# Order of a kernel's first transfers: a weight block ahead of the keys, two more ahead of the values and queries

## The chip, the core and the metric

The kernel runs on one core of a Trainium2 chip. The metric is device time in microseconds (us) of one execution. The engines are named as the profile names them: PE (matmuls, with PEld for its weight loads), DVE, ACT, POOL, and SP, which here issues every DMA.

## The reference, cut to what matters

```python
def _attn_ref(q, k, v, p):                   # 8 batches, 8 heads, 576 tokens, 64 wide; p: 32 rows
    p_packed = sm_attn(p, k, v)              # 32 packed rows attend over keys and values
    out = sm_attn(q, p_packed, p_packed)     # the queries attend over the packed rows
...
x = attn_out, heads side by side             # 4608 x 512
h = x @ w_in                                 # w_in 512 x 1024, float64
solu = h * softmax(h)
ln = (solu - mu) / np.sqrt(var + 1e-06) * g_ln
x = (ln @ w_out).astype(np.float32)          # w_out 1024 x 512, float64
...
logits = x @ w_gate                          # 8 experts, the best one per token
out[mask] = gate_w * (np.maximum(xe @ w1[e], 0.0) @ w2[e])
```

Both w_in and w_out arrive as 64-bit floats: setup_inputs multiplies a float32 draw by a float64 scalar.

## The kernel before

The first half computes attention, h, the normalized solu and its product with w_out, batch by batch (8 batches); the second half runs the experts. Both matrices are fetched as raw words in eight blocks of 1 MB, `raw0` to `raw3` for w_in and `raw4` to `raw7` for w_out, and `decode` (L101 to L118) turns each into float32. A block costs DVE five passes: L111 cuts out sign and exponent, L113 joins them after ACT has shifted the exponent in between (L112), L114 and L115 assemble the mantissa, and L117 multiplies the two. For a block of w_out there follow two scalings and a rounding on ACT (L148, L149) and a subtraction on DVE (L150), which leave a high part `wo_hi` and a low part `wo_lo`.

The attention of a batch is a chain over the engines. `packed` makes scores of the packed rows (`s`, L164), their maxima on DVE (L166), exponentials on ACT (L172), transposes (L178, L181), the sum over the values (L187) and its transpose (L192). `scores2` scores the queries (L225 to L239; POOL scales at L239). `w_keys` multiplies the packed rows by w_in (L212) and splits the result in two on ACT (L213) and DVE (L214). `attnT` transposes the probabilities (L254) and splits them (L256 on ACT, L257 on DVE). `hidden` multiplies both into h, one PSUM tile per 128 tokens and two of those tiles in all (L273, twelve matmuls of 512 columns, a half after the other), takes maxima (L275, L276), exponentials (ACT, L281), the product with h (DVE, L283), squares (L286), and normalizes (L290 to L292). `lnT` transposes (L309 to L312) and `second` multiplies by w_out (L325). A PSUM tile of h comes free when L283 has read it.

For the first batch the order of these steps is written out by hand, in one string at L389. K issues p and the two halves of the keys, V issues the values and queries, F0 to F7 fetch the raw blocks, I0 to I3 and D0 to D3 decode them, and P, S, W, A, H, T, L, C are the steps above (`+` means the next batch). A scheduler then reorders the instructions of each engine, starting from that order, and fixes one order per engine; the engines wait for each other through semaphores. SP's DMAs are all on one queue and share eight completion lanes: the ninth DMA is not issued before the first has landed, and so on.

Of the kernel before, what the change touches and what calls it, by code (L numbers as in the profile page):

```python
# [27 lines left out]
P = 128  # L28
# [13 lines left out]
def fused_kernel(ctx: ExitStack, tc, qT, kT, pT, vm, vt, w_in, w_out, g_ln, w_gate, w1, w2, out):  # L42
    nc = tc.nc
    V, A, G, T, SY = nc.vector, nc.scalar, nc.gpsimd, nc.tensor, nc.sync
# [22 lines left out]
    with ExitStack() as ph:  # L67
# [318 lines left out]
                 "H": hidden, "T": lnT, "X": second, "G": gate, "F": fetch_block, "C": small,  # L386
                 "I": lambda _, i: decode_w_in(i, words[i]), "D": lambda _, i: decode_w_out(i, words[NC + i])}
        done = {("L", 0)}
        for step in ("K F0 F1 V F2 F3 C0 F4 F5 F6 P S0 S1 S2 I0 I1 I2 I3 W F7 A0 L+ H0 H1 D0 D1 T0 T1 D2 D3 A1 A2 C1").split():  # L389
            b = step.count("+")  # L390
            step = step.rstrip("+")
            steps[step[0]](b, *([int(step[1:])] if step[1:] else []))
            done.add((step, b))
# [153 lines left out]
```

## Time and profile before

| | us |
|---|---|
| median of 3 runs | 956.75 |
| lowest and highest | 956.64, 957.22 |
| the profiled execution | 957.72 |
| its span, first to last instruction | 956.0 |
| PE busy in the span | 911.4 |
| DVE busy in the span | 531.5 |

The profiled execution is the one from which every row below comes; 1.72 us of its time lie outside the span. Busy time is a sum over the whole span: it does not say which engine sets the pace of a stretch.

### The profile page before, as it was taken

How to read it: one execution, taken by the hardware profiler on the slowest of the kernel's cores; microseconds unless marked ns; L12 is line 12 of the kernel's file. 1: busy time of each engine (PE TensorE's matmuls, PEld its weight loads, DVE VectorE, ACT ScalarE, POOL GpSimd, SP SyncE). 2: the span in 40 equal slices, each digit the busy share in tenths (PEclk: the TensorE clock that was granted, in tenths of full speed). 3: DMA queues.
4: the chain of work that ended last, by engine and by line, in shares of the span. 5: the costliest groups of instructions: out<-in, count | busy, mean ns of one | idle time of the engine just before them, and what ended most of it. 6: DMA issues, size and time to landing. Idle time of an engine off the chain costs nothing.

```text
span 956.0 us, 18453 instructions
## 1 busy us (share of the span) xinstructions
PE 911.4 (95%) x7480; PEld 806.0 (84%) x7480; DVE 531.5 (56%) x1069; ACT 393.0 (41%) x774; POOL 74.3 (8%) x190
## 2 busy tenths in 40 slices
PE   4469999999999999999999999999999999999997
PEld 1237787887878878788878999999999999999997
DVE  5998667675666757667456253443435353535331
ACT  3366454554555545455345242323333232324230
POOL 0122111120111201112010000000000000000000
PEclk9779999999999999999999999999999999999999
DMA  9713132230322303201007145252535353433411
GB/s 341 273 44 103 51 102 102 58 145 2 103 101 63 140 2 100 101 2 51 2 25 238 54 129 171 85 190 89 178 90 183 94 174 114 155 122 99 130 45 52
DMA packets 41354, 102.89 MB, mean 108 GB/s; under 512 B 4464, under 2 KB 14256, under 8 KB 36144
## 3 DMA queue, kind: packets, MB, share of 16 engines
q1 hardware_dynamic: 41264, 101.65, 31.5%
q8 instruction: 61, 1.00, 0.4%
q14 instruction: 29, 0.24, 0.1%
HBM read 82.60 MB, written 19.04 MB: 106 GB/s over the span
## 4 chain that ended last, share of the span: by engine, by line
PE 89%; DVE 6%; DMA 2%; ACT 1%; issue 1%; SPq 0%; ACTq 0%; DVEq 0%
PE x L325 22%; PE y L468 21%; PE h L450 21%; PE h L273 11%; PE lt L309 3%; PE wb L212 2%; PE s L225 2%; PE lg L336 2%; PE s L164 2%; PE pp L187 1%; PE at L254 1%; DVE raw L115 1%; DVE pw L113 1%; DMA raw<-w_in 1%; DMA raw_0a<-w 1%
## 5 line engine op out<-in xcount | busy, mean ns | idle before, releaser
L325 PE MATMUL x<-lh,wo_hi 128*128 128x320 f32 (+1 forms) x512 | 156.1, 305 | 0.2 <-ACT x L327 0.2
L325 PE MATMUL x<-ll,wo_hi 128*128 128x320 f32 (+1 forms) x512 | 152.6, 298 | 0.0
L325 PE MATMUL x<-lh,wo_lo 128*128 128x320 f32 (+1 forms) x512 | 152.5, 298 | 0.0
L325 PEld LDWEIGHTS x<-lh,wo_hi 128*128 128x128 f32 x512 | 96.7, 189 | 18.8 <-issue 8.7
L325 PEld LDWEIGHTS x<-lh,wo_lo 128*128 128x128 f32 x512 | 96.8, 189 | 2.0 <-issue 0.8
L325 PEld LDWEIGHTS x<-ll,wo_hi 128*128 128x128 f32 x512 | 96.9, 189 | 1.6
L312 DVE TENSOR_TENSOR ll<-lt,lh 128x512 fp32r<-128x512 f32 (+1 forms) x80 | 50.4, 631 | 43.1 <-ACT lh L311 43.0
L273 PE MATMUL h<-wbh,ath 128*128 128x512 f32 (+1 forms) x160 | 67.8, 425 | 1.5 <-DVE e L283 0.8
L275 DVE TENSOR_REDUCE hm<-h 128x1 f32<-128x512 f32 (+1 forms) x80 | 54.5, 685 | 24.8 <-PE h L273 24.3
L273 PE MATMUL h<-wbh,atl 128*128 128x512 f32 (+1 forms) x160 | 65.1, 409 | 0.0
L273 PE MATMUL h<-wbl,ath 128*128 128x512 f32 (+1 forms) x160 | 64.2, 401 | 0.0
L311 ACT CAST lh<-lt 128x512 fp32r<-128x512 f32 (+1 forms) x80 | 43.2, 541 | 46.4 <-PE lt L309 46.1
L481 DVE TENSOR_TENSOR o<-y,gb 128x576 f32<-128x576 f32 (+1 forms) x33 | 24.4, 739 | 67.8 <-PE y L468 61.5
L283 DVE SCALAR_TENSOR_TENSOR e<-e,h 128x1024 f32<-128x1024 f32 (+1 forms) x40 | 48.6, 1216 | 21.1 <-ACT e L281 21.1
L281 ACT ACTIVATE e<-h,hm 128x1024 f32<-128x1024 f32 (+1 forms) x40 | 44.6, 1114 | 26.1 <-DVE hm L276 26.1
L286 ACT ACTIVATE sq<-e,mu 128x1024 bf16<-128x1024 f32 (+1 forms) x40 | 46.0, 1150 | 19.2 <-DVE e L283 14.2
L327 ACT COPY x<-x 128x256 f32<-128x256 f32 (+1 forms) x64 | 25.4, 397 | 57.3 <-PE x L325 56.9
L456 DVE SCALAR_TENSOR_TENSOR hl<-h,hh 128x576 fp32r<-128x576 f32 x64 | 47.9, 749 | 0.3 <-ACT hh L455 0.2
L309 PE MATMUL lt<-ident,e 128*128 128x128 f32 (+1 forms) x320 | 47.2, 267 | 0.5 <-DVE ll L312 0.5
L309 PEld LDWEIGHTS lt<-ident,e 128*128 128x128 f32 (+1 forms) x320 | 35.2, 140 | 9.5 <-issue 3.9
L455 ACT ACTIVATE hh<-h 128x576 fp32r<-128x576 f32 x64 | 41.3, 647 | 0.0
L292 DVE TENSOR_SCALAR e<-e,mu,va 128x1024 f32<-128x1024 f32 (+1 forms) x40 | 32.3, 807 | 11.1 <-POOL va L291 10.4
(229 smaller groups left out, 2090.7 us busy)
## 6 DMA issues: line engine op xcount, KB each, us to landing
k<-kT SPq DMA_DIRECT2D x16, 576.0 KB
q<-qT SPq DMA_DIRECT2D x8, 1152.0 KB
x2s<-x SPq DMA_DIRECT2D x8, 1152.0 KB
x<-x2s SPq DMA_DIRECT2D x8, 1152.0 KB
yT<-o SPq DMA_DIRECT2D x31, 288.0 KB
v<-vm SPq DMA_DIRECT2D x8, 1024.0 KB
raw<-w_in SPq DMA_DIRECT2D x4, 1024.0 KB
raw<-w_out SPq DMA_DIRECT2D x4, 1024.0 KB
```

The costliest lines, as they stand in the source:

```text
L273: T.matmul(ps[:rows, cols], s[x][:, t, g, :rows], s[y][:, g, cols], start=(n == 0), stop=(n == len(passes) - 1))
L275: V.tensor_reduce(nm[:rows, hf : hf + 1], ps[:rows, cols], axis=AX.X, op=ALU.max, negate=True)
L281: A.activation(er, psr, AF.Exp, bias=nm[:rows, 0:1], accum_out=z[:rows])
L283: V.scalar_tensor_tensor(er, er, 1.0 / FF, psr, op0=ALU.mult, op1=ALU.mult, accum_out=mu[:rows])
L286: A.activation(sq[:rows], er, AF.Square, bias=mu[:rows], scale=-float(FF), accum_out=va[:rows])
L309: T.transpose(ps[:, fc, :rows], e[:rows, (f0 + fc) * P : (f0 + fc + 1) * P], ident[:rows, :rows])
L311: A.copy(hi, ps[:, :, :rows])
L312: V.tensor_sub(s["ll", part][:, f0 : f0 + 4, t0 - p0 : t0 - p0 + rows], ps[:, :, :rows], f32(hi))
L325: T.matmul(ps[:, :pn], w[:, fc, cols], s[x, part][:, fc, :], start=(n == 0), stop=(n == 3 * NF - 1))
L450: T.matmul(ps[:, hf, :HALF], w[:, dc, :], x[:, dc, hf * HALF : (hf + 1) * HALF], start=(n == 0), stop=(n == 3 * NC - 1))
L456: V.scalar_tensor_tensor(lo, ps[:, :, :HALF], 0.0, f32(hi), op0=ALU.max, op1=ALU.subtract)
L468: T.matmul(ps[:, hf, :HALF], w[:, fc % 4, :], x[fc][:, hf, :], start=(n == 0), stop=(n == 3 * NF - 1))
```

## The change

The string at L389 gets another beginning. The first block of w_in is fetched ahead of p and the keys, and the second and third ahead of the values and queries; from F3 on the string is what it was.

```diff
-        for step in ("K F0 F1 V F2 F3 C0 F4 F5 F6 P S0 S1 S2 I0 I1 I2 I3 W F7 A0 L+ H0 H1 D0 D1 T0 T1 D2 D3 A1 A2 C1").split():
+        for step in ("F0 K F1 F2 V F3 C0 F4 F5 F6 P S0 S1 S2 I0 I1 I2 I3 W F7 A0 L+ H0 H1 D0 D1 T0 T1 D2 D3 A1 A2 C1").split():
```

Since a scheduler orders each engine's instructions anew, the change moves more than DMAs. On DVE, the start of the program (`s` are the scores of the packed rows, `pw` and `raw` belong to the decoding of a block; the difference, - before and + after):

```order
 L383 MEMSET lg 128x64
+L111 TENSOR_SCALAR pw_334<-raw_129 128x1024
+L113 SCALAR_TENSOR_TENSOR pw_334<-raw_129,pw_334 128x1024
 L166 TENSOR_REDUCE nm_0_158<-s_0_0_0_159 128x1
+L114 TENSOR_SCALAR raw_129<-raw_129 128x1024
+L115 SCALAR_TENSOR_TENSOR raw_129<-raw_129 128x1024
 L166 TENSOR_REDUCE nm_0_158<-s_0_0_1_165 128x1
+L117 SCALAR_TENSOR_TENSOR w_in_sb<-raw_129,pw_334 128x1024
 L168 TENSOR_TENSOR nm_0_158<-nm_0_158 128x1
-L111 TENSOR_SCALAR pw_334<-raw_135 128x1024
+L111 TENSOR_SCALAR pw_341<-raw_137 128x1024
 L174 SCALAR_TENSOR_TENSOR z_0_173<-z_0_173 128x1
```

The whole decoding of the first block now stands around the first maxima, where before it began after them.

On DVE, the place where the split of the first batch's `w_keys` ends (`wbl`, L214) and that of its transposed probabilities begins (`atl`, L257); before:

```order
L214 TENSOR_TENSOR wbl_363<-wb_0_1_378,wbh_362 128x512
L150 TENSOR_TENSOR wo_lo<-raw_150,wo_hi 128x1024
L117 SCALAR_TENSOR_TENSOR raw_152<-raw_152,pw_487 128x1024
L113 SCALAR_TENSOR_TENSOR pw_528<-raw_154,pw_528 128x1024
L214 TENSOR_TENSOR wbl_363<-wb_1_1_385,wbh_362 128x512
L257 TENSOR_TENSOR atl_395<-at_0_396,ath_394 128x512
L114 TENSOR_SCALAR raw_154<-raw_154 128x1024
L150 TENSOR_TENSOR wo_lo<-raw_152,wo_hi 128x1024
L111 TENSOR_SCALAR pw_539<-raw_392 128x1024
```

and after:

```order
L150 TENSOR_TENSOR wo_lo<-raw_152,wo_hi 128x1024
L117 SCALAR_TENSOR_TENSOR raw_154<-raw_154,pw_528 128x1024
L238 RECIPROCAL z_0_2_329<-z_0_2_329 64x8
L113 SCALAR_TENSOR_TENSOR pw_539<-raw_392,pw_539 128x1024
L214 TENSOR_TENSOR wbl_363<-wb_0_1_378,wbh_362 128x512
L214 TENSOR_TENSOR wbl_363<-wb_1_1_385,wbh_362 128x512
L114 TENSOR_SCALAR raw_392<-raw_392 128x1024
L150 TENSOR_TENSOR wo_lo<-raw_154,wo_hi 128x1024
L115 SCALAR_TENSOR_TENSOR raw_392<-raw_392 128x1024
L257 TENSOR_TENSOR atl_395<-at_0_396,ath_394 128x512
```

More of the decoding of w_out (`raw_150`, `raw_152`, `raw_154`, `raw_392` are its four blocks) now stands ahead of the L214s, and ahead of the first L257.

On DVE again, a little further on, up to the first two L283; before:

```order
L117 SCALAR_TENSOR_TENSOR raw_392<-raw_392,pw_539 128x1024
L283 SCALAR_TENSOR_TENSOR e_0_431,mu_0_434<-e_0_431,h_0_414 128x1024
L283 SCALAR_TENSOR_TENSOR e_1_462,mu_1_465<-e_1_462,h_1_445 128x1024
L174 SCALAR_TENSOR_TENSOR z_0_580<-z_0_580 128x1
L175 RECIPROCAL rz_563<-z_0_580 128x1
L290 TENSOR_SCALAR va_0_436<-va_0_436,hz_0_432 128x1
L292 TENSOR_SCALAR e_0_431<-e_0_431,mu_0_434,va_0_436 128x1024
L275 TENSOR_REDUCE hm_2_753<-h_2_752 128x1
L150 TENSOR_TENSOR wo_lo<-raw_392,wo_hi 128x1024
```

and after:

```order
L117 SCALAR_TENSOR_TENSOR raw_392<-raw_392,pw_539 128x1024
L275 TENSOR_REDUCE hm_0_415<-h_0_414 128x1
L275 TENSOR_REDUCE hm_1_446<-h_1_445 128x1
L166 TENSOR_REDUCE nm_0_565<-s_1_0_0_566 128x1
L257 TENSOR_TENSOR atl_395<-at_2_557,ath_394 128x2x64
L275 TENSOR_REDUCE hm_0_415<-h_0_414 128x1
L150 TENSOR_TENSOR wo_lo<-raw_392,wo_hi 128x1024
L276 TENSOR_TENSOR hm_0_415<-hm_0_415 128x1
L275 TENSOR_REDUCE hm_1_446<-h_1_445 128x1
L166 TENSOR_REDUCE nm_0_565<-s_1_0_1_572 128x1
L276 TENSOR_TENSOR hm_1_446<-hm_1_446 128x1
L168 TENSOR_TENSOR nm_0_565<-nm_0_565 128x1
```

The two L283 follow directly behind the last of these rows. The last L150 stood behind them and now stands ahead of them, and the maxima of h (L275), which were mixed with decoding before, now stand behind it.

## Rows read from the trace of the kernel before

**Rows 1.** The page, busy time of the span and DVE's busy tenths in 40 slices

```profile
PE 911.4 (95%) x7480; PEld 806.0 (84%) x7480; DVE 531.5 (56%) x1069; ACT 393.0 (41%) x774; POOL 74.3 (8%) x190
...
DVE  5998667675666757667456253443435353535331
```

**Rows 2.** PE's waits, 100 to 956 us: total, times, longest; the costliest

```profile
PE lgt L342 <- ACT lg L337: 0.9, 6, 0.2
```

**Rows 3.** Stages: PE, PEld, DVE, ACT, POOL busy; clock, DMA share, GB/s

```profile
0.00:5.00 5.00, 0.00 (x0) 0.00 (x0) 1.08 (x14) 1.59 (x2) 0.68 (x6) 1.00 0.50 145
5.00:10.00 5.00, 2.37 (x16) 0.43 (x16) 1.07 (x3) 0.68 (x3) 0.00 (x0) 1.00 1.04 385
10.00:15.00 5.00, 3.44 (x21) 1.32 (x21) 3.83 (x8) 3.22 (x6) 0.00 (x0) 1.00 1.06 406
...
20.00:25.00 5.00, 3.68 (x84) 2.47 (x83) 3.79 (x7) 2.10 (x4) 0.00 (x0) 1.00 1.02 410
```

**Rows 4.** Timeline of PE, its first matmuls: start, length, what, idle before

```profile
5.56 1.19 PE L164 MATMUL s<-k,p 64*32 64x288 f32 x8 [5.56 <-DMA k<-kT]
```

**Rows 5.** Timeline of DVE, six places

```profile
10.19 0.69 DVE L111 TENSOR_SCALAR pw<-raw 128x1024 uint16<-128x1024 uint16 x1 [0.96 <-DMA raw<-w_in]
...
47.23 0.92 DVE L237 TENSOR_SCALAR z<-z 64x8 f32<-64x8 f32 x1
...
49.92 0.63 DVE L214 TENSOR_TENSOR wbl<-wb,wbh 128x512 fp32r<-128x512 f32 x1
...
68.95 1.20 DVE L283 SCALAR_TENSOR_TENSOR e<-e,h 128x1024 f32<-128x1024 f32 x1
...
73.44 0.81 DVE L292 TENSOR_SCALAR e<-e,mu,va 128x1024 f32<-128x1024 f32 x1 [0.68 <-POOL va L291]
...
74.77 1.22 DVE L150 TENSOR_TENSOR wo_lo<-raw,wo_hi 128x1024 fp32r<-128x1024 f32 x1
```

**Rows 6.** Stages 52 to 75 us, columns as in rows 3

```profile
52.00:58.00 6.00, 5.38 (x14) 4.01 (x15) 6.00 (x8) 4.05 (x6) 2.42 (x1) 0.50 0.49 175
58.00:64.00 6.00, 5.54 (x33) 2.83 (x32) 6.00 (x10) 3.48 (x5) 0.00 (x0) 1.00 0.00 0
64.00:68.00 4.00, 0.00 (x0) 0.00 (x0) 4.00 (x9) 1.35 (x3) 0.06 (x1) 1.00 0.00 0
69.60:75.00 5.40, 5.40 (x15) 4.23 (x16) 3.71 (x10) 5.40 (x10) 0.97 (x4) 0.50 0.00 0
```

**Rows 7.** Timeline of PE, two starts after idle time

```profile
69.59 1.17 PE L178 MATMUL a1t<-ident,a 128*128 128x128 f32 x4 [5.71 <-ACT a L172]
...
82.77 0.45 PE L273 MATMUL h<-wbh,ath 128*64 128x512 f32 x1 [0.76 <-DVE e L283]
```

**Rows 8.** DVE's groups, 0 to 75 us: busy us, mean ns

```profile
L115 DVE SCALAR_TENSOR_TENSOR raw<-raw 128x1024 f32<-128x1024 uint32 x8 | 9.7, 1214 | 0.1
L113 DVE SCALAR_TENSOR_TENSOR pw<-raw,pw 128x1024 uint16<-128x1024 uint16 x8 | 9.7, 1207 | 2.2 <-ACT pw L112 2.2
L114 DVE TENSOR_SCALAR raw<-raw 128x1024 int32<-128x1024 int32 x8 | 5.4, 681 | 0.0
L111 DVE TENSOR_SCALAR pw<-raw 128x1024 uint16<-128x1024 uint16 x8 | 5.4, 681 | 1.0 <-DMA raw<-w_in 1.0
L117 DVE SCALAR_TENSOR_TENSOR w_in_sb<-raw,pw 128x1024 f32<-128x1024 f32 x4 | 4.9, 1218 | 0.0
L150 DVE TENSOR_TENSOR wo_lo<-raw,wo_hi 128x1024 fp32r<-128x1024 f32 x4 | 4.8, 1208 | 0.0
```

**Rows 9.** Timeline of POOL, two of the first batch's three L239

```profile
46.90 1.22 POOL L239 TENSOR_TENSOR a<-a,z 128x512 f32<-128x512 f32 x1 [2.99 <-DVE z L238]
50.13 4.29 POOL L239 TENSOR_TENSOR a<-a,z 64x256 f32<-64x256 f32 x1 [2.01 <-ACT pw L112]
```

**Rows 10.** The chain that ended last, two stretches of L273: start, us

```profile
70.97 4.73 PE h L273 x12
77.83 2.77 PE h L273 x12
```

## The prediction

> **What bounds the kernel now.** The page comes first: PE is busy 95% of the span, but DVE's tenths show 5 to 9 in the first three slices, some 70 us, and little later [rows 1]. PE's waits after 100 us hold nothing larger than 0.9 us in total on one line [rows 2], so what the change can give or take lies in the first 100 us. The stages show who sets the pace there. DVE idles 3.9, 3.9, 1.2 and 1.2 us in the slices 0 to 5, 5 to 10, 10 to 15 and 20 to 25 us, 10.2 us together, while the DMA engines are full from 5 us on [rows 3]. PE gets its first half of the keys at 5.56 us [rows 4], and DVE its first block of w_in at 10.19 us [rows 5]. After 25 us DVE has no gap up to 68 us (its busy column equals the slice in the rows shown [rows 6]). At 68.95 us comes the first L283, which frees a PSUM tile of h [rows 5]. From 69.59 us PE is busy almost without a gap; only at 82.77 us does it wait 0.76 us, for the L283 that frees the next tile [rows 7]. So the time follows from one question: when has PE, in the same work, passed the first L283s, and how fast does it run then.
>
> **Step 1, the landings.** The first 5 us moved 145 GB/s, 0.73 MB; the next 5 us moved 385 [rows 3]. A block of 1.05 MB therefore takes 2.72 us. Put ahead of the keys it moves their first half from 5.56 to at most 8.3 us. A large transfer at the head should also fill the slow first microseconds; I estimate 0.7 us of that, so 7.6 us (bounds 6.9 and 8.3). The block itself carries 0.39 MB more than p and the half of the keys that landed at 5.56: 1.0 us more, less about 1.2 for the quicker start, gives 5.4 us (4.9 to 6.6).
>
> **Step 2, DVE up to the L214s.** A decode pass takes 0.60 us (L111, L114) or 1.14 us (L113, L115, L117, L150) from start to start: the means of 0.68 and 1.21 less the 0.07 to 0.08 by which a row overlaps the next [rows 8]. DVE now idles to 5.4 us, but for 1.1 us of memsets, 4.3 us. Twice an L113 stands directly behind its L111 and waits 1.2 us for ACT, as the one in 20 to 25 us did [rows 3], 2.5 us in all. The first maximum needs PE 1.25 us after the keys, so at 8.85, 0.4 us after the first L113 ends. The L174 and the second L113 wait about 0.65 and 0.9 us behind two exponentials and an L112 on ACT. Sum 8.75 against 10.2: 1.5 us gained, of the 4.8 us by which the block comes sooner.
>
> The third L214 began at 49.92 us [rows 5]. Nine more instructions of decoding stand ahead of it now: two L111 or L114 (1.2), one L115, two L113, two L117, two L150 (7 x 1.14 = 8.0), together 9.2 us. DVE and POOL also hold each other up. An L237 took 0.92 us and ended with POOL's L239 [rows 5, 9], where the tiny operation needs 0.07; before there were two such waits, 1.8 us. In the new order one L237 stands behind an L239 again (0.9 us), and an L150 starts while POOL is in another. Of whether that L150 waits I know only the bounds: 0, or the 0.7 us left of the L239. I take 0.7, as the L237's row is nearest; so 0.2 us less than before. L214 then starts at 49.9 + 9.2 - 1.5 - 0.2 = 57.4 us.
>
> The Trainium skill, SBUF — State Buffer, section "Who interferes with whom", says that a DVE instruction with two SBUF inputs and a GpSimd instruction that reads SBUF exclude each other, the later one fully blocked. The trace agrees in the one direction: the smaller L239 took 4.29 us while an L150, an L117 and an L113 followed each other on DVE [rows 9]. By that rule the 0.7 us are certain, and the sum stays as it is.
>
> **Step 3, from the L214s to the first L283.** Work that hid PE's part is now spent earlier. Two L214, an L114, an L150 and an L115 take DVE to 61.5, the first L257 to 62.2 us; only then can PE finish the first halves of h, 8 matmuls, then a transpose and scores, then 6 matmuls of second halves. On slow PE a matmul costs 0.43 us (4.73 us for 12, the last two fast), on fast PE 0.23 (2.77 for 12) [rows 10]. That is 3.4 + 1.1 + 2.6 = 7.1 us or 1.9 + 0.7 + 1.4 = 4.0 us. Then L275 and L276 with the last L150 between them, 1.9 us, and ACT's exponential, 1.3 us: the first L283 starts at 72.5 on slow PE. On fast PE the sum gives 69.4; DVE, which has its own 12 us since 57.4, gives 69.6 to 69.9. The clock was 1.2 GHz up to 58 us and 2.4 GHz after it; PE's stretch of h had begun about 5.5 us earlier, and the next rise, at 75 us, came 5.5 us after 69.6 [rows 6, 7]. Here PE works from 58.1 us on, with a gap of some 0.7 us before 62.2: a rise at 63.6 or at 67.7 us. I take the middle: first L283 at 71.1 us, 2.1 us later than the 68.95 of before. The L150 that stood at 74.77 us is done by then.
>
> **Step 4, behind the first L283.** Before, PE had stood from 64 us on, its clock fell, and the work from 69.6 to 75.0 us ran at 0.50 [rows 6]: 2.7 us lost. Now PE stands only about 2 us between the scores and the L283's end, so I take the clock to stay up. PE would then be ready for the h tile at 82.77 earlier, and DVE decides: the first L292 follows L283 by 4.5 us (73.44 - 68.95 [rows 5]), the second by 2.5 more, and two L275, two L312, two L166 and the next L283 add 4.4: 11.4 us behind the first L283, not 13.8. That is 82.5 us. Against 82.77 it is 0.3 us early, but two things are owed: six transposes of the next batch (0.65 us on fast PE), which PE had done by then, and a wait of about 0.45 us for the last L312, which the values' product used to cover. Sum: -0.3 + 0.65 + 0.45 = **+0.8 us**. Against the profiled span that is 956.8 us, with the 1.72 us around it 958.5; the median lies 0.97 us below the profiled execution, so **957.5 us**.
>
> **The rivals.**
> *PE stays slow (slower).* If the new gaps keep the clock at 1.2 GHz past the first L283, that comes at 72.5 to 73.5 us and the slow stretch behind it is not regained: 73 - 68.95 less 0.9 us of step 4 that does not hang on the clock gives +3.1 us, 959.9 us. It decides from the point where no rise comes before about 69 us. For it: step 3 exposes PE with a gap right before its matmuls. Against it: both rises came within 5.5 us of sustained work.
> The Trainium skill, TensorE: Matmul & The Clock Gate, section "HAM oscillation — how this bites in real kernels", says that waits between groups of matmuls throw the clock back so that each group starts slow; by that this rival would hold, and [rows 6] show one such fall, after an idle stretch twice as long as the one expected here.
> *The head start is kept (faster).* DVE sets the pace to 68 us, and the block lands 4.8 us sooner. If DVE kept that and PE followed, the first L283 would come near 64 us and some 4 us be gained: 952.8 us. Against it: step 2 finds only 1.5 us, and 9.2 us of decoding have moved ahead of the L214s on which PE waits.
> *Nothing changes at the end (no change).* The same decoding has to be done before `second` can run, and PE is bound behind it: 956.75 us. For it: nothing is removed or added, only moved.
>
> **How the numbers follow.** My forecast has 0.58, slow PE 0.22, the kept head start 0.10, no change 0.10. The forecast's own range is 956.0 (first L283 at 69.6 us) to 959.0 (72.5). The range 955.2 to 960.0 reaches to the slow rival and leaves out the head start and the ends. About 0.2%, 1.9 us, is what a measurement of this kernel tells from no change. All of the head start and 0.02 of the forecast lie on the fast side, 0.12; slow PE and 0.06 of the forecast on the slow side, 0.28; the rest, 0.60, within.
>
> **What would show it.** Step 1: first matmul of scores near 7.6 us, first L111 near 5.4. Step 2: third L214 near 57.4, DVE idle near 8.8 us before 25. Step 3: DVE no longer full between 63 and 71 us, first L283 near 71. Step 4: PE at the full clock behind it, and h matmuls of the fifth tile near 82.5. The prediction fails if the scheduler's new order costs or saves PE more than 1 us after 100 us, where I count nothing, or if the clock takes another course than I assume.

## The result, and the profile after

The changed kernel takes 969.04 us (median of 4 runs, 967.5 to 969.39), beside 956.89 us for the kernel before on the same chip: a ratio of 1.0122, 95% interval 1.0107 to 1.0137. That is 12.2 us slower; 957.5 us was predicted. The profiled execution took 968.97 us, its span 967.2 us, 11.2 more than before.

The page of the changed kernel, busy time and DVE's tenths, beside [rows 1]:

```profile
PE 916.5 (95%) x7480; PEld 807.7 (84%) x7480; DVE 532.8 (55%) x1069; ACT 392.2 (41%) x774; POOL 75.0 (8%) x190
...
DVE  6987667566675756757456243353535353435331
```

PE does the same 7480 matmuls and is busy 5.1 us longer; the rest of the 11.2 us it stands idle. Up to the first L283, at 72 us, it went much as predicted. The timeline of DVE, beside [rows 5]:

```profile
5.83 0.69 DVE L111 TENSOR_SCALAR pw<-raw 128x1024 uint16<-128x1024 uint16 x1 [3.92 <-DMA raw<-w_in]
...
51.99 1.01 DVE L237 TENSOR_SCALAR z<-z 64x8 f32<-64x8 f32 x1
...
57.10 1.27 DVE L214 TENSOR_TENSOR wbl<-wb,wbh 128x512 fp32r<-128x512 f32 x2
...
58.90 1.63 DVE L150 TENSOR_TENSOR wo_lo<-raw,wo_hi 128x1024 fp32r<-128x1024 f32 x1
...
72.18 1.22 DVE L283 SCALAR_TENSOR_TENSOR e<-e,h 128x1024 f32<-128x1024 f32 x1
```

And of PE, beside [rows 4, 7]:

```profile
8.04 1.19 PE L164 MATMUL s<-k,p 64*32 64x288 f32 x8 [8.04 <-DMA k<-kT]
...
73.46 0.50 PE L273 MATMUL h<-wbh,ath 128*128 128x512 f32 x1 [2.50 <-DVE e L283]
...
84.30 0.45 PE L273 MATMUL h<-wbh,ath 128*64 128x512 f32 x1
```

The h tile that began at 82.77 us now begins at 84.30. Most of the loss arises later. The stages (columns as in [rows 3]):

```profile
58.00:64.00 6.00, 5.43 (x16) 4.01 (x17) 6.00 (x7) 2.01 (x3) 1.45 (x2) 0.50 0.01 3
64.00:68.00 4.00, 4.00 (x18) 2.16 (x18) 1.91 (x4) 2.69 (x4) 0.00 (x0) 0.62 0.00 0
...
73.70:77.20 3.50, 3.50 (x12) 2.84 (x12) 2.38 (x7) 3.11 (x8) 1.03 (x4) 0.52 0.00 0
84.00:156.00 72.00, 70.94 (x732) 57.36 (x729) 48.34 (x107) 37.77 (x83) 11.10 (x31) 1.00 0.29 101
156.00:162.60 6.60, 3.91 (x34) 1.33 (x32) 6.60 (x17) 3.62 (x8) 1.77 (x3) 1.00 0.50 180
162.60:169.40 6.80, 6.80 (x46) 3.17 (x39) 3.35 (x9) 3.11 (x7) 1.61 (x2) 0.50 0.01 4
```

From 84 to 156 us PE is as busy as ever. Then DVE is full for 6.6 us, PE busy for 3.91 of them, and behind that its clock falls to 1.2 GHz for 6.8 us. What PE waits for there, in its timeline:

```profile
157.08 0.66 PE L309 MATMUL lt<-ident,e 128*128 128x128 f32 x4 [1.00 <-DVE ll L312]
157.68 2.01 PE L212 MATMUL wb<-w_in_sb,ppc 64*32 64x512 f32 x16
161.03 0.66 PE L309 MATMUL lt<-ident,e 128*128 128x128 f32 x4 [1.34 <-DVE ll L312]
162.03 2.53 PE L212 MATMUL wb<-w_in_sb,ppc 64*32 64x512 f32 x16 [0.34 <-DVE wbl L214]
```

The two traces can be compared exactly. The order that the scheduler gave PE differs from the 124th to the 1208th matmul instruction, and from there on not at all, on no engine. Behind the 178th, the 864th and the 1208th instruction both orders have gone through the same set. The start of the next matmul in the timeline of PE (us), in both kernels and in the four of the first experiment:

| matmul instruction | before | after | x1 | x2 | x3 | x4 |
|---|---|---|---|---|---|---|
| 1st | 5.56 | 8.04 | 8.34 | 5.69 | 8.13 | 5.52 |
| 179th | 75.63 | 78.48 | 77.59 | 80.78 | 78.33 | 74.57 |
| 865th | 167.28 | 177.23 | 169.38 | 178.08 | 169.96 | 174.09 |
| 1209th | 214.56 | 225.76 | 216.66 | 226.72 | 217.24 | 222.64 |

Of the 11.2 us at the 1209th, 2.85 are lost by the 179th, 7.1 between there and the 865th, 1.25 behind it. The prediction counted nothing in the last two stretches.

### The profile page after: what moved, and what is told of

It is laid out like the page before. It is cut to its first block, busy times and chain, and to the rows that moved or that the text cites. A ratio compares the mean times of both kernels' runs of the same rounds, so it can differ in the third digit from the quotient of the medians.

```text
span 967.2 us, 18457 instructions
## 1 busy us (share of the span) xinstructions
PE 916.5 (95%) x7480; PEld 807.7 (84%) x7480; DVE 532.8 (55%) x1069; ACT 392.2 (41%) x774; POOL 75.0 (8%) x190
## 4 chain that ended last, share of the span: by engine, by line
PE 88%; DVE 7%; DMA 2%; ACT 1%; issue 1%; SPq 0%; POOL 0%; ACTq 0%; DVEq 0%
PE h L450 21%; PE y L468 21%; PE x L325 21%; PE h L273 11%; PE lt L309 3%; PE wb L212 2%; PE s L225 2%; PE lg L336 2%; PE s L164 2%; PE pp L187 1%; DVE raw L115 1%; PE at L254 1%; DMA raw_0a<-w 1%; DVE pw L113 1%; DMA k<-kT 1%; PE a1t L178 1%
## 5 line engine op out<-in xcount | busy, mean ns | idle before, releaser
L325 PE MATMUL x<-lh,wo_hi 128*128 128x320 f32 (+1 forms) x512 | 156.3, 305 | 0.9 <-ACT x L327 0.6
L325 PE MATMUL x<-ll,wo_hi 128*128 128x320 f32 (+1 forms) x512 | 152.9, 299 | 0.0
L325 PE MATMUL x<-lh,wo_lo 128*128 128x320 f32 (+1 forms) x512 | 152.2, 297 | 0.0
L325 PEld LDWEIGHTS x<-lh,wo_hi 128*128 128x128 f32 x512 | 96.9, 189 | 18.2 <-issue 8.7
L325 PEld LDWEIGHTS x<-ll,wo_hi 128*128 128x128 f32 x512 | 96.9, 189 | 2.9 <-issue 1.3
L325 PEld LDWEIGHTS x<-lh,wo_lo 128*128 128x128 f32 x512 | 96.8, 189 | 1.1
L312 DVE TENSOR_TENSOR ll<-lt,lh 128x512 fp32r<-128x512 f32 (+1 forms) x80 | 50.4, 630 | 43.1 <-ACT lh L311 43.0
L275 DVE TENSOR_REDUCE hm<-h 128x1 f32<-128x512 f32 (+1 forms) x80 | 54.7, 686 | 30.5 <-PE h L273 29.9
L273 PE MATMUL h<-wbh,ath 128*128 128x512 f32 (+1 forms) x160 | 67.7, 424 | 2.5 <-DVE e L283 2.5
L273 PE MATMUL h<-wbh,atl 128*128 128x512 f32 (+1 forms) x160 | 65.2, 410 | 0.6 <-DVE atl L257 0.6
L273 PE MATMUL h<-wbl,ath 128*128 128x512 f32 (+1 forms) x160 | 64.2, 401 | 0.0
L283 DVE SCALAR_TENSOR_TENSOR e<-e,h 128x1024 f32<-128x1024 f32 (+1 forms) x40 | 48.6, 1217 | 21.3 <-ACT e L281 21.1
L309 PE MATMUL lt<-ident,e 128*128 128x128 f32 (+1 forms) x320 | 47.7, 271 | 3.2 <-DVE ll L312 3.2
L309 PEld LDWEIGHTS lt<-ident,e 128*128 128x128 f32 (+1 forms) x320 | 35.5, 142 | 14.3 <-DVE ll L312 6.2
L212 PE MATMUL wb<-w_in_sb,ppc 64*32 64x512 f32 x256 | 32.2, 677 | 8.1 <-DVE wbl L214 4.1
```

Of the source, the lines that this page charges most:

```text
L212: T.matmul(ps[c * NP : (c + 1) * NP, :], s["pp"][r, c, :], w_in_sb[r, c, cols], start=True, stop=True)
L273: T.matmul(ps[:rows, cols], s[x][:, t, g, :rows], s[y][:, g, cols], start=(n == 0), stop=(n == len(passes) - 1))
L275: V.tensor_reduce(nm[:rows, hf : hf + 1], ps[:rows, cols], axis=AX.X, op=ALU.max, negate=True)
L283: V.scalar_tensor_tensor(er, er, 1.0 / FF, psr, op0=ALU.mult, op1=ALU.mult, accum_out=mu[:rows])
L309: T.transpose(ps[:, fc, :rows], e[:rows, (f0 + fc) * P : (f0 + fc + 1) * P], ident[:rows, :rows])
L312: V.tensor_sub(s["ll", part][:, f0 : f0 + 4, t0 - p0 : t0 - p0 + rows], ps[:, :, :rows], f32(hi))
```

## The experiments

**Transfers or order?** The change does two things: other landings, and a new order of instructions. A table of runs (first instruction + count, in the order of the code) and this function hold an engine to a given order, so that the two can be crossed; line numbers are 21 higher in these kernels:

```diff
+def pin_orders(tc):
+    for engine, order in ORDERS.items():
...
+        for first, then in zip(rows, rows[1:]):
+            tc.add_manual_dep(then, first.name, mybir.DependencyInfo(mybir.DependencyClass.NoSync, mybir.DependencyReason.DATA),
+                              reason="order")
```

x1: the changed string, PE, DVE, ACT and POOL in the order of before.

> The changed order of the first transfers, but PE, DVE, ACT and POOL are held to the instruction order that the kernel before has. Theory A (the loss comes from the new order of the instructions, not from when the first data land): 957 to 960 us, at most the 2.5 us by which the first scores start later (8.04 against 5.56 us) above 956.9. Theory B (the loss comes from the transfers themselves, the late keys and what follows on the DMA queue): 965 to 970 us, as the changed kernel.

x2: the old string, the four engines in the changed order.

> The first transfers as before, but the four engines are held to the instruction order of the changed kernel. Theory A (instruction order): 966 to 972 us; the first DVE passes now wait for a block that lands late, so it may be a little slower than the changed kernel. Theory B (the transfers): 957 to 959 us.

x3: the changed string and order up to the 178th matmul instruction, then the old order.

> The changed kernel up to the 178th matmul instruction of PE (78.5 us, and the matching places on DVE, ACT and POOL, where both kernels have done the same set of instructions); from there on the instruction order of the kernel before. At that place the changed kernel is 2.85 us late. Theory A (the larger part of the loss is the later order, batches 1 and 2): 959.5 to 960.5 us, 956.9 plus 2.85. Theory C (the late start itself throws the later batches off, whatever their order): 966 to 969 us.

x4: the old string and order up to there, then the changed order.

> The mirror image: the kernel before up to the 178th matmul instruction of PE (75.6 us), then the instruction order of the changed kernel. Theory A: 956.9 plus the 8.7 us that the changed kernel loses behind that place, 964 to 967 us. Theory C: 956.5 to 958 us.

Measured, against 957.25 us: x1 959.96 (1.0028, 1.0016 to 1.0039), x2 970.17 (1.0141, 1.0124 to 1.0158), x3 960.6 (1.0031, 1.0019 to 1.0042), x4 966.57 us (1.0100, 1.0083 to 1.0117). Theory A holds in all four (x3 ended 0.1 us above its range): the new transfers under the old order cost 2.7 us, the new order behind the 178th instruction alone 9.3 us with the old transfers. The whole new order with the old transfers costs 12.9 us (x2), so the two parts do not simply add up. The table above shows the same inside one execution: from the 179th to the 865th x1 and x3, in the old order, take 91.8 and 91.6 us like the kernel before (91.7), x2 and x4 97.3 and 99.5 (the changed kernel 98.8). Holding the engines to an order costs nothing of its own there: from the 179th to the 1209th x1 and x3 take 139.1 and 138.9 us, the kernel before 138.9.

**Which half of the change?**

```diff
-"F0 K F1 F2 V F3
+"F0 K F1 V F2 F3      (e1)
+"K F0 F1 F2 V F3      (e2)
```

> Half of the change: only the first block ahead of the keys (the string begins F0 K F1 V F2). The scheduler's order from batch 1 on is that of the changed kernel but for a few rows. Theory A (the order decides): 966 to 970 us. A theory by which each of the two moves costs its own share: about 960 to 963 us.

> The other half: the keys stay first, only the third block moves ahead of the values and queries (K F0 F1 F2 V). The order from batch 1 on is again nearly that of the changed kernel, and the keys land as before. Theory A: 963 to 968 us. By shares: 959 to 963 us, and with the first half of the change the two would add up to 12 us.

e1 took 969.99 us (1.0134, 1.0115 to 1.0153; its four runs lie between 965.64 and 972.07), e2 966.87 us (1.0100, 1.0083 to 1.0117). Of the 12.2 us of the whole change the first half costs 12.5, the second 9.4. They do not add up, as costs of landings would: either is enough to tip the order into nearly the same one. Of the 1350 matmul records between the 179th and the 1209th instruction, 1267 (e1) and 1199 (e2) stand in the same place as in the changed kernel; in the kernel before it is 370.

**A row on ACT?** In the changed order the scaling of packed rows that are needed two batches later stands ahead of the exponentials of h, and ACT stands in it until their DMA lands. ACT's timeline, changed kernel:

```profile
140.51 0.31 ACT L123 ACTIVATE p<-p 128x128 f32<-128x128 f32 x1 [3.00 <-DMA p<-pT]
140.73 1.09 ACT L281 ACTIVATE e<-h,hm 128x1024 f32<-128x1024 f32 x1
```

and before, where it stands behind the first of them:

```profile
130.83 0.31 ACT L123 ACTIVATE p<-p 128x128 f32<-128x128 f32 x1 [0.61 <-DMA p<-pT]
```

x5, ACT's rows of the changed kernel (x6 moves the row the other way in the kernel before):

```diff
-L123 p (batch 4)
 L281 e (batch 1, tile 2)
 ...
 L281 e (batch 1, tile 3)
+L123 p (batch 4)
```

> The changed kernel with one row moved on ACT: the scaling of the packed rows of batch 4 (L123), which stands in ACT's order for 3.0 us while its DMA lands (137.5 to 140.5 us), moves from ahead of the exponentials of h (L281, batch 1, tiles 2 and 3) to behind both; every other row is held to the order of the changed kernel. Theory D (this wait starves DVE and PE from 140 to 163 us and so brings the idle time and the fall of the clock at 162.6 us): 962 to 965 us. Theory E (the order of PE's own work is to blame, the row on ACT is not): 968 to 970 us.

> The kernel before with the same row moved the other way: L123 of batch 4 one place sooner, ahead of the exponential of tile 2 of batch 1, as the changed kernel has it. Theory D: ACT stands about 2 us and the time rises by 2 to 6 us, 959 to 963 us. Theory E: 956.5 to 958 us.

x5 took 967.28 us (1.0097, 1.0080 to 1.0114), 1.8 less than the changed kernel; x6 958.63 (1.0010, 1.0000 to 1.0019), 1.1 more than before, although ACT stood 3.16 us in it. Both lie between the ranges of the two theories. The row costs little, and x5's interval still overlaps the changed kernel's (1.0107 to 1.0137). As the cause of the waits and of the clock's fall theory D fell: with the wait on ACT gone PE still waits at the same place in x5 (PE's waits, 84 to 226 us: total, times, longest),

```profile
PE lt L330 <- DVE ll L333: 2.3, 2, 1.3
PE wb L233 <- DVE wbl L235: 1.2, 2, 0.8
```

and its clock falls at 162.0 us.

**Where in the order?** Four kernels change over elsewhere.

x9a, changed order up to 110.3 us, then the old one:

> The changed kernel up to 110.3 us of its trace (436 matmul instructions of PE; w_keys of batch 1 not yet finished, of the product with w_out of batch 0 the whole second part, 96 matmuls, still to come), behind it what is left in the order of the kernel before. Theory F (the loss arises because PE spends the matmuls of the second part of batch 0 too early, between 110 and 144 us, and has none left to cover the chain of batch 2 at 150 to 170 us): 960 to 962 us, as the kernel that goes over at 78 us. Theory H (batch 1's chain stands 7 to 10 us later by then, and that alone fixes the loss): 965 to 969 us.

x9c, the same at 143.6 us:

> The same with the switch at 143.6 us of the changed kernel's trace (632 matmul instructions), when the last matmul of the second part of batch 0 has been issued; behind it the order of the kernel before. PE has hardly waited up to there (0.4 us since 84 us) and its clock is up. Theory F (the cover is spent by then, although PE has lost nothing yet): 964 to 968 us. Theory G (the order of the rows from 144 to 170 us is what is wrong): 960 to 962 us.

x16, old order up to 107.1 us, then the changed one:

> The mirror image of the switch at 110 us: the kernel before up to 107.1 us of its trace (436 matmul instructions; w_keys of batch 1 done), behind it what is left in the order of the changed kernel. Theory H (the loss is fixed where batch 1's chain falls behind, between 78 and 110 us): 957.5 to 960 us. Theory G' (the changed order behind 107 us loses by itself): 963 to 967 us, as the kernel that takes the changed order from 76 us on.

x17, changed order up to 93.2 us, then the old one:

> The changed kernel up to 93.2 us of its trace (299 matmul instructions; the sum over the values of batch 1 done, its scores of the queries and its w_keys still to come), behind it what is left in the order of the kernel before. Between the switch at 78 us (960.6 us) and the one at 110 us (965.8 us). If the rows from 93 to 110 us, with batch 1's scores and w_keys put behind the product with w_out, are the loss (theory H): 960.5 to 962 us. If the rows from 78 to 93 us are: 964 to 966 us.

x9a 965.8 us (1.0086, 1.0070 to 1.0101), x9c 967.18 (1.0099, 1.0084 to 1.0115), x16 964.8 (1.0079, 1.0062 to 1.0096), x17 963.21 us (1.0057, 1.0041 to 1.0074). x9c: going back to the old order at 144 us did not undo the loss, although PE had hardly waited by then; F's range holds and G's does not, but x9c also has waits of its own behind the switch, the longest 2.51 us for DVE's L233. x16: the rows behind 107 us lose 7.4 us by themselves, so it is not batch 1's late chain alone, as theory H has it. x9a missed theory F's range and lies in theory H's; its trace shows why in part: the old order has nothing left to put between batch 1's groups of w_keys, and PE waits at the seam (timeline of PE),

```profile
111.98 1.06 PE L233 MATMUL wb<-w_in_sb,ppc 64*32 64x512 f32 x8 [0.75 <-DVE wbl L235]
...
114.56 1.09 PE L275 MATMUL at<-ident,a 128*128 128x128 f32 x4 [0.94 <-DVE wbl L235]
```

with the clock at 1.2 GHz from 114.2 to 117.7 us. x17 lies between its two ranges, and has a wait of 1.9 us for L190 of its own. A kernel that changes over in the middle pays for the seam, so these four bound the place and do not price it.

**The cover.** What differs where PE waits is what stands beside w_keys of batch 2. The matmuls of L325 in that stretch, before (first number the stretch; PE busy, count):

```profile
147.86:155.83 7.97, 3.38 (x24) 2.99 (x24) 1.00 0.81 297
```

and after:

```profile
157.68:164.50 6.82, 0.00 (x0) 0.00 (x0) 0.86 0.37 156
```

Before, 24 matmuls of the product with w_out stand between steps that need DVE; after, none. x14 takes just these 24 out of there in the kernel before and issues them behind the gate of batch 0:

```diff
 L225 s (batch 2)
 L212 wb (batch 2)
-L325 x2 (batch 1, first quarter) x24, in two pieces
 ...
 L342 lgt (batch 0)
+L325 x2 (batch 1, first quarter) x24
```

> The kernel before, all rows in its own order except 24 matmuls of PE: the first quarter of the product with w_out of batch 1 (L325, x2_1_0_0), which stands between the w_keys groups of batch 2 at 148.9 to 152.4 us, stands behind the gate of batch 0 (158.6 us) instead. The same work, without the cover. Theory K (the later order costs time where PE has only steps of the chain over DVE and ACT to do and no product with w_out between them): PE stands in waits of 2 to 3 us on DVE and ACT that were covered, 959 to 961.5 us, up to 963 with a fall of the clock. Theory L (DVE's own load of that stretch sets the pace, cover or not): 956.5 to 958 us.

959.06 us (1.0024, 1.0013 to 1.0035): 1.6 us slower with the same work, as theory K has it, at its lower end. Inside its profiled execution the stretch from the 179th to the 865th matmul takes 94.3 us, against 91.7. Its stage from 147 to 153 us and the waits in it (timeline of PE):

```profile
147.00:153.00 6.00, 4.12 (x40) 1.63 (x38) 5.97 (x17) 3.64 (x8) 1.92 (x2) 1.00 0.89 312
```

```profile
149.86 0.63 PE L330 MATMUL lt<-ident,e 128*128 128x128 f32 x4 [1.40 <-DVE ll L333]
...
152.20 0.66 PE L330 MATMUL lt<-ident,e 128*128 128x128 f32 x4 [0.34 <-DVE ll L333]
```

The waits are of the kind of the changed kernel: L309 stands until DVE, full, has come to its L312.

**The clock.** x10 fills the two waits of the changed kernel with matmuls that are issued again:

```diff
-            for i, (t0, tn) in enumerate(tl):
+            for i, (t0, tn) in enumerate(tl * (3 if (b, pr) == (2, 2) else 1)):
...
-                    for c in range(NC):
+                    for c in list(range(NC)) * (2 if (b, hf, g) == (2, 0, 1) else 1):
                         T.matmul(ps[c * NP : (c + 1) * NP, :], s["pp"][r, c, :], w_in_sb[r, c, cols], start=True, stop=True)
```

> The changed kernel in its own order, with 12 matmul instructions of batch 2 issued once more (8 of the scores of the queries' last tile, 4 of the second group of w_keys), which rewrite the same PSUM values; they fill 1.0 us each of the two waits of PE that begin at 156.1 and 159.7 us. Theory I (the clock falls at 162.6 us because PE stands in these waits; the fall costs half its 6.8 us): no fall there, 965 to 966.5 us. Theory J (the clock's fall does not hang on these waits): 968.5 to 970 us, and the row of the clock falls as before.

967.64 us (1.0103, 1.0088 to 1.0119), between the two ranges and 1.4 less than the changed kernel, which the intervals do not tell from nothing. In its profiled execution the clock does not fall (stages as above):

```profile
156.00:162.60 6.60, 5.70 (x58) 2.43 (x59) 6.60 (x19) 3.39 (x8) 1.78 (x3) 1.00 0.51 182
162.60:169.40 6.80, 6.55 (x65) 4.35 (x54) 4.91 (x19) 3.35 (x9) 1.62 (x2) 1.00 0.00 1
```

That is as theory I has it, but one execution does not prove it. The profiled execution of e2 goes through the same stage, with the same two waits of 1.00 and 1.34 us unfilled, and its clock stays up (stages 3.13 us earlier than those of the changed kernel, and PE's timeline):

```profile
152.87:159.47 6.60, 3.91 (x34) 1.33 (x32) 6.60 (x17) 3.62 (x8) 1.78 (x3) 1.00 0.51 180
159.47:166.27 6.80, 6.55 (x68) 4.48 (x61) 5.11 (x21) 3.32 (x8) 1.62 (x2) 1.00 0.02 4
```

```profile
157.90 0.66 PE L309 MATMUL lt<-ident,e 128*128 128x128 f32 x4 [1.34 <-DVE ll L312]
158.90 1.66 PE L212 MATMUL wb<-w_in_sb,ppc 64*32 64x512 f32 x16 [0.34 <-DVE wbl L214]
```

In the other traces with both waits (the changed kernel, e1, x2, x4, x5) the clock falls at the second or up to 2.1 us after its end. So these waits can bring it down and do not always do so. Half of 6.8 us was in any case too high a price. The 865th instruction of the changed kernel comes at 174.34 us in x10, 2.9 sooner, and a new wait takes 1.4 of that back (timeline of PE):

```profile
203.52 0.41 PE L346 MATMUL x<-lh,wo_hi 128*128 128x320 f32 x1 [1.36 <-ACT x L348]
```

x15 does the same with the gap of 5.7 us in the kernel before [rows 7]:

```diff
+            if (b, t) == (0, 1):
+                ps = psx.tile([P, 512], F32, name="busy", tag="x")
+                for _ in range(22):
+                    T.matmul(ps, s["at_hi"][:, 0, 0, :], s["wb_hi"][:, 0, 0:512], start=True, stop=True)
```

> The kernel before in its own order, with 22 matmuls of 128 x 512 whose product nobody reads, put into the 5.7 us in which PE stands at 63.9 to 69.6 us. Theory I (a wait of PE brings the clock down behind it, here from 68.3 to 75.1 us, and half of that stretch is the price): no fall there, PE 2 to 2.7 us ahead at 75 us, 954 to 956 us unless the exponentials of h set the pace there. Theory M (the fall is paid back by the wait of 0.8 us at 82.8 us and by DVE's order, as a part of it was in the changed kernel with its waits filled): 956 to 957.5 us.

958.32 us (1.0010, 1.0001 to 1.0019): nothing gained. In the profiled execution the clock did not fall at 68 us, but further on PE waited 2.07 us where it had waited 0.76, for an L283 (L304 here), and the clock fell there, from 82.5 to 85.9 us (timeline of PE):

```profile
63.54 5.30 PE L318 MATMUL busy<-wbh,ath 128*128 128x512 f32 x22
...
82.52 0.69 PE L294 MATMUL h<-wbh,ath 128*64 128x512 f32 x1 [2.07 <-DVE e L304]
```

Theory M holds in its mechanism; its range ended 0.8 us too low.

**A version that beats both?** e2's profiled execution, the fastest of its four, came to the 179th matmul 0.95 us ahead of the kernel before (74.68 us). x11 joins e2's string and its order up to there to the old order behind:

```diff
-"K F0 F1 V F2 F3
+"K F0 F1 F2 V F3
...
+    pin_orders(tc)
```

> Only the third block ahead of the values and queries, in the order that this string gets up to 74.7 us (178 matmul instructions of PE); behind it the order of the kernel before. The string alone came to that place 0.95 us sooner than the kernel before (74.68 against 75.63 us), with the clock up since 61.7 us, and lost 9 us behind it. Theory A (the order behind 76 us is the loss): 955.5 to 957 us, level with or a little below the kernel before. Theory C (an early start throws the later batches off whatever their order): 963 to 967 us.

960.58 us (1.0033, 1.0021 to 1.0044), 6.3 less than e2 and 3.2 more than before. All seven runs (959.1 to 963.75) miss theory A's range, and their median is not in theory C's either. The profiled one is the slowest of them: there the clock fell at 70.2 and again at 87.3 us, which it had not in e2's, and the 179th came at 77.26 us. Why the other six miss the range is not shown. No kernel here beats the one before.

## Why the prediction was wrong

**Step 1, the landings: right.** The first scores came at 8.04 us (7.6, bounds 6.9 to 8.3), the first block's L111 at 5.83 (5.4).

**Step 2, DVE up to the L214s: right, in part because two errors cancel.** The third L214 began at 57.10 us, 57.4 forecast. DVE idled 7.7 us before 25 us, where 8.75 was the sum, and 1.3 us between 25 and 58 us, where nothing was counted; together the early block gained 1.3 us (1.5 forecast). The L237 was held again, 1.01 us long; the L150 behind POOL's L239 took 1.63 instead of 1.21 us, so the wait, bounded by 0 and 0.7 us, was 0.4. POOL's two L239 ended at 59.44 us, 0.54 us after that L150 began at 58.90:

```profile
53.30 6.14 POOL L239 TENSOR_TENSOR a<-a,z 128x512 f32<-128x512 f32 x2 [0.32 <-DVE z L238]
```

That this L150 was held as well agrees with SBUF — State Buffer, section "Who interferes with whom", of the Trainium skill. The 0.7 us that the prediction called certain by it were too many.

**Step 3, the first L283: in its range.** 72.18 us, 71.1 forecast (69.6 to 72.5). Of the two moments given for the clock's rise, 63.6 and 67.7 us, it was the later.

**Step 4: wrong by 2 us.** "I take the clock to stay up" failed: PE stood 2.50 us for the first L283, and ran at 0.52 from 73.7 to 77.2 us. The tile forecast at 82.5 us came at 84.30; with the transposes owed, 2.85 us were lost at the 179th matmul where +0.8 was the sum. In part this is what the slow rival described, although the clock had risen once, at 67 us. Had the kernel kept the old order from there, it would have taken 960.6 us (x3), near that rival's 959.9 us.

**What failed for good is the count of nothing behind 100 us.** From PE's waits in the kernel before [rows 2] the prediction concluded that the change can give or take only in the first 100 us. It named this as a way to be wrong and left it without a chance or a price. The order of PE was changed up to the 1208th matmul instruction, far past the rows that were weighed, and x4 shows that this order alone costs 9.3 us. The mistake was to read "PE is busy without a gap" as "there is nothing to lose": PE is busy there because the product with w_out of the batch before covers a chain over DVE and ACT, and an order can spend that cover early. The changed kernel does: batch 1's first scores of queries start at 100.81 us instead of 90.93, the second part of batch 0's product is used up by 143.6 us, and when batch 2's chain comes DVE is full and PE has nothing else.

Shown are the order as the cause (x1 to x4, e1, e2) and the missing cover as a mechanism (x14, 1.6 us for 24 matmuls). The row on ACT (x5, 1.8 us) and the filled waits (x10, 1.4 us) lie at the edge of what their intervals tell, and that the waits bring down the clock is likely and not shown. e2 tells the order from the clock: in nearly the same order and without a fall its profiled execution takes 96.5 us from the 179th to the 865th, so 4.8 of the 7.1 us lost there need no slow clock.

The parts do not add up to 9.3 us. Between the 179th and the 865th the changed kernel has 2.0 us more idle time than the kernel before, and 3.4 us are half of the slow stretch. Much of the 1.7 us left lies on `w_keys` (L212). Eight of its matmuls take 1.06 us when they stand alone. Sixteen, two groups of eight, take hardly more in the kernel before, where both groups run side by side (timeline of PE, batches 1 and 2):

```profile
101.53 1.09 PE L212 MATMUL wb<-w_in_sb,ppc 64*32 64x512 f32 x16
...
152.35 1.09 PE L212 MATMUL wb<-w_in_sb,ppc 64*32 64x512 f32 x16
```

In the changed kernel one group starts ahead of the other, and the sixteen take longer:

```profile
108.67 1.74 PE L212 MATMUL wb<-w_in_sb,ppc 64*32 64x512 f32 x16
...
157.68 2.01 PE L212 MATMUL wb<-w_in_sb,ppc 64*32 64x512 f32 x16
```

In e2, at the full clock, all L212 of these two batches take 7.5 us, against 6.4 in the kernel before. What remains after these 1.1 us is not settled. Nor is it known why the scheduler tips into the other order.

**The rivals.** The kept head start and no change did not happen: all that DVE gained by the early block was spent before the L283s, on the decoding that step 2 moved ahead of the L214s. The slow rival has the right sign and is 9 us too small; its clock is not what lost most of the time.

## What to carry to other kernels

Where a scheduler re-sorts, an edit is not local: compare the whole order on each engine down to the place where it is the same again, and ask of each engine that is never idle what covers it, and whether the new order spends the cover sooner. To learn what an edit costs, cross its two effects: new transfers in the old order, old transfers in the new order. Here the old order, pinned under the new transfers, took 959.96 us where the scheduler's own order took 969.04. Half the length of a slow stretch of PE was more than what its absence gave back in x10 and x15 (1.4 us and nothing, where half was 3.4 us each), because a wait for ACT (x10) or for DVE (x15) grew further on.

## What the runs showed of the hardware

The clock fell at 162.6 us although PE had been busy in 70.94 of the 72 us up to 156 us, and no single wait behind that was longer than 1.34 us. With 5.70 instead of 3.91 busy us in the stage ahead of it, it stayed up (x10); but it stayed up as well in e2's trace, with 3.91 busy us and the same waits. What decides between the two is not known. TensorE: Matmul & The Clock Gate, section "HAM oscillation — how this bites in real kernels", of the Trainium skill tells of such falls behind long waits for data, with half of the slow time as the price. Here it fell behind short waits, and with the fall gone the time was lower by 1.4 us, where half would be 3.4.

The granted clock reads 1.00 in every trace up to its first recorded change, and that reading is not to be trusted: four transposes L178 take 1.17 us at 22.79 us in the changed kernel (column 1.00), as long as at 69.59 us in the kernel before (0.50) [rows 7].

```profile
22.79 1.17 PE L178 MATMUL a1t<-ident,a 128*128 128x128 f32 x4 [4.73 <-ACT a L172]
```

Executions of one program can differ by more than a small effect: e1's four runs span 6.4 us, the kernel before's 13 in the same comparison 2.0. Only one of e1's was traced, so whether the clock's course makes the difference is not shown.
